# Attention decode on one core: the last K chunk loaded ahead of V, the last quarter of V multiplied in turned form, the output summed in one PSUM bank on four column groups

## Chip, cores and metric

One core of one Trainium2 chip. The metric is device time in microseconds (us) of the whole program; a run is one execution. Positions below are in us from the start of the span, which is the time from the first to the last instruction of the profiled execution and is some 1.8 us shorter than the reported time. Before the change the median of three runs was 1277.08 us (1277.07 to 1277.14).

Engines: PE does matrix products (PEld is its weight load), DVE is the vector engine, ACT the scalar engine, POOL the general one, and SP issues most DMAs ("SPq" is its queue).

## The reference, cut to what matters

```python
# x [1,1,448]; k_cache, v_cache [1, 8, 65536, 256] bf16; wq [448, 4096]; wo [4096, 448]
g = sigmoid((x * gate_w).sum(-1))
q = (x @ wq)                          # 16 heads of 256; two heads share one of 8 K/V heads
p = softmax(q . k * 256**-0.5)        # over 65536 positions
a = (p @ v).reshape(1, 1, 4096) @ wo  # [448]
b = mixer(layernorm(x))               # rank-one MLP, 14 blocks of 128 features, bias b2
out = g * a + (1 - g) * b
```

K and V are 268 MB each, and each byte is used once. Everything else is small.

## The kernel before

K and V of each head pair arrive in 8 chunks of 4 MB, K and V alternating, into a ring of four buffers, on SP's queue. Of a chunk, four steps of 1 MB: DVE turns (transposes) a K step, PE multiplies it with the query (8 products of 512 columns). After four steps ACT takes the exponential of the scores, DVE turns it, and PE multiplies V in 32 products, each with 4 columns of weights, on four column groups of PE that write four partition groups of one PSUM bank.

```python
    def load(item):                       # items: K0, V0, K1, V1, ... chunks of the stream
        ...
        elif item == 2 * total - 1:       # last K and V chunk: in pieces of SB = 16 blocks
            for s in range(last - 1):
                piece(item - 1, s * SB, SB)                     # K quarters 0, 1, 2
            piece(item, 0, SB)                                  # V quarter 0
            piece(item - 1, (last - 1) * SB, SB)                # K quarter 3
            for s in range(1, last - 1):
                piece(item, s * SB, SB)                         # V quarters 1, 2
            tail = SB // 2 - 2
            piece(item, (last - 1) * SB, SB - tail)             # V quarter 3, 10 blocks
            piece(item, last * SB - tail, tail)                 # and 6 blocks
    ...
    def p_v(i, s, lo=0, hi=SB // 2):      # 8 products for a V quarter
        ...
            nc.tensor.matmul(
                pv[g % 2][32 * a:32 * a + 4, :], lhsT=pT[:, k, :, s], rhs=vt[:, j * DH:(j + 2) * DH],
                start=first and k < 4, stop=last and k >= SB // 2 - 4, tile_position=(0, 32 * a))
    ...
    def o_scale(g):                       # evacuate and divide by the softmax sum
        nc.vector.tensor_scalar(out=pvs[:], in0=pv[g % 2][:], scalar1=rden[:, 0:1], ...)
    def o_turn(g):                        # add the four groups and turn: 4 fp32 products
        ...
        nc.vector.tensor_copy(out=oT[:], in_=o_ps)
    def o_out(g):                         # 4 products of 1x448, then added to an SBUF row by DVE
        ...
        nc.vector.tensor_tensor(out=dst[:], in0=acc[:], in1=a_ps, op=ALU.add)
    ...                                   # the end, after the last chunk's softmax
        for s in range(sizes[c]):
            p_v(i, s)                     # the last step in two parts, 10 and 6 blocks
        o_scale(HKV - 1)
    o_turn(HKV - 1)
    o_out(HKV - 1)
    nc.sync.dma_start(out=out[0, 0].rearrange("(o n) -> o n", o=1), in_=res[:])
```

(Comments are mine; the loop's end is shown with its conditions left out.) The mixer's 14 blocks run between the steps, each ending in one 1x448 product and one DVE accumulation into the same SBUF row.

The softmax here doesn't subtract the row's maximum and nothing guards it: scores larger than these inputs give would overflow.

## Time and profile before

| | before |
|---|---|
| time | 1277.08 us |
| span of the profiled run | 1275.1 us |
| HBM read | 544 MB, 427 GB/s over the span |
| PE, DVE busy | 59%, 52% |
| last byte of V landed | 1268.66 |
| last landing to end of span | 6.45 us |

The page divides the span into 40 equal slices; a digit of the DMA row is the busy share of the DMA engines in tenths, the GB/s row what they moved.

```profile
DMA  9999999999999999999999999999999999999996
GB/s 393 434 431 430 436 432 427 436 433 430 435 430 430 433 434 432 432 434 428 433 435 427 435 433 430 432 434 430 431 435 431 430 433 435 430 433 435 428 433 276
```

The stream is busy from start to end. Only the first and the last slice leave clear room, so a gain is to be looked for there first (a digit 9 means 90% or more, so this is a pointer and no proof). The end of the stream is the place to read closely. Here is the timeline of the kernel before. Columns: start, duration (both us), engine, line of the kernel, operation, output<-inputs, partitions x elements out<-in, how many instructions the row merges; in brackets, how long the engine sat idle before it and what released it.

```profile
1260.91 2.31 DVE L346 STREAM_TRANSPOSE kT_184<-ring_72 128x2048 f32<-128x2048 f32 x1 [1.36 <-DMA ring_72<-in_A_k_cache_dram]
1263.28 1.89 PE L354 MATMUL sc_75<-kT_184,qw 128*128 128x512 bf16 x8 [1.78 <-DVE kT_184 L346]
...
1265.21 0.60 ACT L361 ACTIVATE p_186<-sc_75 128x512 bf16<-128x512 f32 x1 [12.98 <-PE sc_75 L354]
...
1265.93 0.71 DVE L365 STREAM_TRANSPOSE pT_188<-p_186 128x512 bf16<-128x512 bf16 x1 [2.71 <-ACT p_186 L361]
...
1267.05 2.04 PE L376 MATMUL pv_77<-ring_73,pT_188 128*4 128x512 bf16 x32
...
1268.71 0.09 PEld L376 LDWEIGHTS <-pT_188 128*4 128x4 bf16 x2 [0.26 <-issue]
1269.14 0.75 DVE L393 TENSOR_SCALAR pvs<-pv_77,rden 128x512 f32<-128x512 f32 x1 [1.61 <-PE pv_77 L376]
...
1269.94 1.05 PE L402 MATMUL misc<-sel,pvs 128*128 128x2 f32 x8 [0.85 <-DVE pvs L393]
1271.03 0.16 DVE L406 CAST oT<-misc 128x4 bf16<-128x4 f32 x1 [1.15 <-PE misc L402]
...
1271.25 0.92 PE L412 MATMUL misc<-wo_97,oT 128*1 128x448 bf16 x4 [0.25 <-DVE oT L406]
1272.20 0.61 DVE L417 TENSOR_TENSOR res<-acc,misc 1x448 bf16<-1x448 f32 x1 [1.01 <-PE misc L412]
1272.84 0.32 SPq L452 DMA_DIRECT2D out_dram<-res  x1
```

Read it downwards. The last K quarter is turned as soon as it lands (1260.91, released by the DMA), its scores, exponential and turn follow, and the 32 products with V start at 1267.05. The last two weight loads (1268.71) come after a pause, 0.05 us after the last V blocks landed (1268.66, below). The view names no releaser here; that they waited for these blocks is read from the times. From there everything is in series: scaling, turn (8 passes), cast, four products, addition, output DMA.

Each DMA of 128 partitions is spread over 16 rings and its semaphore is raised once by each. From these records in the trace, for each piece of the last chunk, when the fastest and the slowest ring had landed it (a consumer that needs the whole piece waits for the slowest):

```
piece            before: fastest, slowest   after: fastest, slowest
K quarter 3          1253.49  1260.79          1251.16  1258.77
V quarter 0          1251.00  1258.32          1253.64  1261.23
V quarter 1          1255.93  1263.79          1256.09  1263.67
V quarter 2          1258.37  1266.22          1258.52  1266.24
V quarter 3, end     1260.85  1268.66          1261.01  1268.68
```

### The profile page before, as it was taken

How to read it: one execution, taken by the hardware profiler on the slowest of the kernel's cores; microseconds unless marked ns; L12 is line 12 of the kernel's file. 1: busy time of each engine (PE TensorE's matmuls, PEld its weight loads, DVE VectorE, ACT ScalarE, POOL GpSimd, SP SyncE). 2: the span in 40 equal slices, each digit the busy share in tenths (PEclk: the TensorE clock that was granted, in tenths of full speed). 3: DMA queues.
4: the chain of work that ended last, by engine and by line, in shares of the span. 5: the costliest groups of instructions: out<-in, count | busy, mean ns of one | idle time of the engine just before them, and what ended most of it. 6: DMA issues, size and time to landing. Idle time of an engine off the chain costs nothing.

```text
span 1275.1 us, 10091 instructions
## 1 busy us (share of the span) xinstructions
PE 758.4 (59%) x4374; PEld 288.1 (23%) x4374; DVE 661.7 (52%) x429; ACT 62.7 (5%) x159; POOL 83.1 (7%) x118
## 2 busy tenths in 40 slices
PE   3564656655566556656557565575655655656656
PEld 2121222212222222222122122221222222222212
DVE  7364455554464644646445455464453644545545
ACT  0000000000000000000000000000000000000000
POOL 3111012110021100210000000000000000000000
PEclk9888888888889887898888888788887888879789
DMA  9999999999999999999999999999999999999996
GB/s 393 434 431 430 436 432 427 436 433 430 435 430 430 433 434 432 432 434 428 433 435 427 435 433 430 432 434 430 431 435 431 430 433 435 430 433 435 428 433 276
DMA packets 21154, 544.88 MB, mean 427 GB/s; under 512 B 2675, under 2 KB 2806, under 8 KB 3958
## 3 DMA queue, kind: packets, MB, share of 16 engines
q1 hardware_dynamic: 19730, 540.55, 98.5%
q0 software_dynamic: 1376, 3.69, 0.8%
q8 instruction: 34, 0.56, 0.2%
q14 instruction: 10, 0.08, 0.0%
q10 hardware_dynamic: 4, 0.00, 0.0%
HBM read 544.22 MB, written 0.00 MB: 427 GB/s over the span
## 4 chain that ended last, share of the span: by engine, by line
DMA 64%; DVE 17%; PE 17%; issue 2%; DVEq 0%; SPq 0%; ACT 0%; ACTq 0%
DMA ring_70<-in_A_k_cache_dram 58%; PE sc_74 L354 14%; DVE kT_183 L346 9%; DVE kT_184 L346 7%; DMA ring_72<-in_A_k_cache_dram 6%; PE sc_75 L354 1%; PE misc L402 1%; DVE acc L337 1%; PE misc L412 1%; PE misc L325 0%; DVE acc L417 0%; PE pv_77 L376 0%; DVE pT_188 L365 0%; DVE oT L406 0%; DVEq L346 0%
## 5 line engine op out<-in xcount | busy, mean ns | idle before, releaser
L354 PEld LDWEIGHTS <-qw 128*128 128x128 bf16 x2048 | 222.3, 111 | 772.5 <-issue 324.5
L354 PE MATMUL sc_74<-kT_183,qw 128*128 128x512 bf16 x512 | 190.8, 536 | 239.6 <-DVE kT_183 L346 239.6
L346 DVE STREAM_TRANSPOSE kT_183<-ring_70 128x2048 f32<-128x2048 f32 x64 | 147.6, 2306 | 166.6 <-DMA ring_70<-in_A_k_cache_dram 146.7
L354 PE MATMUL sc_75<-kT_183,qw 128*128 128x512 bf16 x512 | 145.7, 433 | 114.7 <-DVE kT_183 L346 114.7
L346 DVE STREAM_TRANSPOSE kT_183<-ring_72 128x2048 f32<-128x2048 f32 x64 | 147.0, 2297 | 114.3 <-DMA ring_72<-in_A_k_cache_dram 91.7
L354 PE MATMUL sc_74<-kT_184,qw 128*128 128x512 bf16 x512 | 150.9, 445 | 25.4 <-DVE kT_184 L346 25.4
L346 DVE STREAM_TRANSPOSE kT_184<-ring_72 128x2048 f32<-128x2048 f32 x64 | 145.7, 2277 | 4.9 <-PE sc_75 L354 3.4
L346 DVE STREAM_TRANSPOSE kT_184<-ring_70 128x2048 f32<-128x2048 f32 x64 | 145.6, 2275 | 2.8 <-PE sc_74 L354 2.7
L354 PE MATMUL sc_75<-kT_184,qw 128*128 128x512 bf16 x512 | 131.7, 401 | 18.1 <-DVE kT_184 L346 18.1
L365 DVE STREAM_TRANSPOSE pT_187<-p_185 128x512 bf16<-128x512 bf16 x32 | 22.8, 712 | 103.4 <-ACT p_185 L361 103.4
L365 DVE STREAM_TRANSPOSE pT_188<-p_186 128x512 bf16<-128x512 bf16 x32 | 22.8, 712 | 86.7 <-ACT p_186 L361 86.7
L361 ACT ACTIVATE p_185<-sc_74 128x512 bf16<-128x512 f32 x32 | 19.1, 597 | 713.4 <-PE sc_74 L354 713.4
L376 PE MATMUL pv_77<-ring_71,pT_187 128*4 128x512 bf16 x512 | 30.4, 379 | 24.4 <-DVE pT_187 L365 24.4
L376 PE MATMUL pv_76<-ring_71,pT_187 128*4 128x512 bf16 x512 | 30.4, 379 | 24.4 <-DVE pT_187 L365 24.4
L376 PEld LDWEIGHTS <-pT_187 128*4 128x4 bf16 x1024 | 22.1, 86 | 87.3 <-DVE pT_187 L365 64.6
L376 PE MATMUL pv_77<-ring_73,pT_188 128*4 128x512 bf16 x512 | 30.6, 379 | 18.3 <-DVE pT_188 L365 18.3
L376 PE MATMUL pv_76<-ring_73,pT_188 128*4 128x512 bf16 x512 | 30.4, 379 | 18.3 <-DVE pT_188 L365 18.3
L361 ACT ACTIVATE p_186<-sc_75 128x512 bf16<-128x512 f32 x32 | 19.1, 597 | 449.5 <-PE sc_75 L354 449.5
L376 PEld LDWEIGHTS <-pT_188 128*4 128x4 bf16 x1024 | 22.1, 86 | 71.5 <-DVE pT_188 L365 48.4
L337 DVE SCALAR_TENSOR_TENSOR acc<-misc,half_g,acc 1x448 f32<-1x448 f32 x14 | 9.4, 672 | 53.1 <-PE misc L325 53.1
L314 POOL TENSOR_SCALAR t_b<-t_b 128x448 f32<-128x448 f32 x14 | 7.9, 567 | 361.3 <-ACT t_b L306 361.3
L139 POOL DMA_DIRECT2D wo_97<-in_A_wo_dram x4 | 3.1, 784 | 295.4 <-PE misc L412 295.4
(90 smaller groups left out, 201.9 us busy)
## 6 DMA issues: line engine op xcount, KB each, us to landing
ring_70<-in_A_k_cache_dram SPq DMA_DIRECT2D x32, 4096.0 KB, 26.5
ring_71<-in_A_v_cache_dram SPq DMA_DIRECT2D x32, 4096.0 KB, 29.8
ring_72<-in_A_k_cache_dram SPq DMA_DIRECT2D x31, 4096.0 KB, 29.4
ring_73<-in_A_v_cache_dram SPq DMA_DIRECT2D x31, 4096.0 KB, 33.9
ring_72<-in_A_k_cache_dram SPq DMA_DIRECT2D x4, 1024.0 KB, 27.5
ring_73<-in_A_wq_dram SPq DMA_DIRECT2D x1, 3072.0 KB, 10.4
ring_73<-in_A_v_cache_dram SPq DMA_DIRECT2D x3, 1024.0 KB, 26.9
wo_96<-in_A_wo_dram POOLq DMA_DIRECT2D x4, 448.0 KB, 15.1
```

The costliest lines, as they stand in the source:

```text
L139: nc.gpsimd.dma_start(out=wo_t[g % 2][:], in_=A_wo[g * 512:(g + 1) * 512, :].rearrange("(q p) n -> p q n", p=128),)
L314: nc.gpsimd.tensor_scalar(out=t_b[:], in0=t_b[:], scalar1=GELU_C1, scalar2=1.0, op0=ALU.mult, op1=ALU.add)
L337: nc.vector.scalar_tensor_tensor(out=acc[:], in0=misc[0:1, 0:D], scalar=half_g[0:1, 0:1], in1=acc[:], op0=ALU.mult, op1=ALU.add,)
L346: nc.vector.transpose(out=kT[n % 2][:].bitcast(FP32), in_=kn[:, s * SB * 128:(s + 1) * SB * 128])
L354: nc.tensor.matmul(sc[i % 2][:], lhsT=qw[:, g, q, PAD - s:PAD - s + 128], rhs=kv[:, :, q // 2, :, q % 2], start=(s == 0 and q == 0), stop= ...
L361: nc.scalar.activation(out=p_t[i % 2][:], in_=sc[i % 2][:], func=ACT.Exp, scale=scale, accum_out=den[g % 2][:, c:c + 1],)
L365: nc.vector.transpose(out=pT_t[i % 2][:], in_=p_t[i % 2][:])
L376: nc.tensor.matmul(pv[g % 2][32 * a:32 * a + 4, :], lhsT=pT[:, k, :, s], rhs=vt[:, j * DH:(j + 2) * DH], start=first and k < 4, stop=last ...
L402: nc.tensor.matmul(o_ps[:, 2 * c:2 * c + 2], lhsT=pvs[:, lo:lo + 128], rhs=sel[:, 2 * half:2 * half + 2], start=(half == 0), stop=(half == 1),
L412: nc.tensor.matmul(a_ps, lhsT=oT[:, 2 * c + r:2 * c + r + 1], rhs=wo_t[g % 2][:, 2 * r + c, :], start=(c == 0 and r == 0), stop=(c == 1 an ...
```

## The change

Intent: the work behind the last V byte should be as short as possible. Five things were done.

1. All of the last K chunk is loaded ahead of V.
2. The last V quarter is multiplied the other way round ("turned"): V's blocks are the weights (128x128) and the two heads' probabilities the two moving columns. The result comes out already turned, and is added in PSUM to the turned sums of all earlier V. So evacuation and turn of the earlier sums can run before the last V quarter lands.
3. Division by the softmax sum moves behind the turn, onto 128x4 values.
4. The output row is summed all along in one PSUM bank, as four rows of 112 in four column groups, so the DVE accumulations go. The bias is broadcast early and added once at the end, and four rows are written out.
5. Query windows are built for one head pair at a time (a smaller clearing at the start).

```diff
@@ load @@
-            for s in range(last - 1):
+            for s in range(last):
                 piece(item - 1, s * SB, SB)
-            piece(item, 0, SB)
-            piece(item - 1, (last - 1) * SB, SB)
-            for s in range(1, last - 1):
+            for s in range(last - 1):
                 piece(item, s * SB, SB)
-            tail = SB // 2 - 2
-            ... 10 and 6 blocks
+            piece(item, (last - 1) * SB, SB - TAIL)      # TAIL = 4
+            piece(item, last * SB - TAIL, TAIL)
@@ gate: the bias rides along in the second column @@
-    nc.tensor.matmul(z_ps, lhsT=one_f[:], rhs=z1[:], start=True, stop=True)
+    nc.tensor.matmul(z_ps, lhsT=one_f[:], rhs=zb[:], start=True, stop=True)
@@ output sum @@
+    def to_acc(col, rows, stop=False):
+        for a in range(4):
+            nc.tensor.matmul(
+                acc[32 * a:32 * a + 1, 0:DQ], lhsT=col, rhs=rows[:, DQ * a:DQ * (a + 1)],
+                start=a not in opened, stop=stop, tile_position=(0, 32 * a),
+            )
+            opened.add(a)
@@ last V quarter @@
+    def p_v_turned(i, s, lo, hi):
+        ...
+        for j in range(lo, hi):
+            for c in range(2):
+                at = (s * SB + j) * DH + c * 128
+                nc.tensor.matmul(
+                    o_ps[:, 2 * c:2 * c + 2], lhsT=vt[:, at:at + 128], rhs=pT[:, j, :, s],
+                    start=False, stop=(j == SB - 1 and c == 1), skip_group_check=True,
+                )
@@ end @@
-    o_turn(HKV - 1)
-    o_out(HKV - 1)
-    nc.sync.dma_start(out=out[0, 0].rearrange("(o n) -> o n", o=1), in_=res[:])
+    nc.vector.tensor_copy(out=pvs[:, 0:DH], in_=pv[g % 2][:, 0:DH])
+    nc.scalar.activation(out=pvs[:, DH:2 * DH], in_=pv[g % 2][:, DH:2 * DH], func=ACT.Copy)
+    o_turn(g)
+    p_v_turned(i, s, 0, SB - TAIL)
+    p_v_turned(i, s, SB - TAIL, SB)
+    nc.vector.tensor_tensor(oT, o_ps, rden, op=ALU.mult)          # 128x4, views left out
+    o_out(g)
+    nc.vector.tensor_scalar(
+        out=res[0:97, :], in0=acc[0:97, 0:DQ], scalar1=bias[0:97, 0:1], scalar2=None, op0=ALU.add
+    )
+    nc.sync.dma_start(out=out[0, 0].rearrange("(a n) -> a n", a=4), in_=res[0:97:32, :])
```

(Cut: the per-head softmax sum, the smaller query windows, and the same steps between head pairs.)

## The prediction

> **What bounds the kernel now.** The page shows 544 MB read at a mean 427 GB/s and DMA at 9 tenths in each of the 40 slices but the last (6 tenths). PE is busy 59%, DVE 52% of the 1275.1 us span. Changes in steady state hide under the stream; only what lies before the first and after the last byte moves the time.
>
> **Head.** The removed 7.04 us clearing of the query window comes before the first K tile, for which DVE still waits at 23.25 us (timeline). I expect nothing.
>
> **Tail of before** (landing records, timeline). The last K quarter lands at 1260.8 and starts a chain: transpose 2.3, scores 1.9, exp 0.7, transpose 0.7 us, then all 32 products with V from 1267.05. The last V blocks land on the slowest engine at 1268.7, so chain and stream end together. Then in series: last products and drain 0.43, scaling of 128x512 0.75, turn 1.05, cast 0.17, four 1x448 products 0.93, addition 0.61, output DMA 2.27, some 0.05 per hand-over: 6.4 us from last landing to end.
>
> **What the change does there.** The last K quarter goes ahead of V0 and lands 2.4 us earlier (1 MB at 427 GB/s); three quarters of V are multiplied as they land, and their evacuation and turn no longer wait for the last bytes. Estimate from the durations above, from the landing of the third V quarter (1266.2, same place in the stream):
> - 8 products and drain 0.8 -> 1267.05
> - DVE copies one half, 128x256: 0.46 (between 0.17 for 128x4 and 0.75 for 128x512) -> 1267.55. ACT copies the other only afterwards (the program makes it wait), under the first half's turn. The Trainium skill, page "PSUM — Partial Sum Buffer", section "PSUM bank collisions raise a hardware error", says why: two engines must not use one bank and quadrant at once.
> - turn 1.05 -> 1268.6
> - 32 turned products (128x128 weights, 2 columns) 0.88, from the query projection's 27.5 ns per pair, drain 0.15 -> 1269.65
> - scaling into oT 0.2 -> 1269.85
> - 16 products of 1x112 in four column groups 0.65, against 0.93. At 28 ns a pair issue limits: the skill's page "TensorEngine Tiling (Array Packing)", section "Instruction Overhead", gives about 60 cycles per matmul, which agrees with 27.5 ns
> - bias addition 97x112 0.3, against 0.61 -> 1270.85
> - output DMA of four 224-byte rows 2.3 -> 1273.1
>
> That is 2.0 us off the span, all on the critical path, all in the last 10 us. The path moves from the stream's last byte to PE's work after the third V quarter: the last 4 blocks (1268.7) are there when PE reaches them.
>
> Off the path, worth nothing: 21 DVE accumulations of 0.6 to 0.7 us removed, scaling moved to ACT, query windows built per head pair, 324 more PE instructions.
>
> **Predicted: 1275.1 us, range 1274.2 to 1276.3.** Chances: faster by over 2% 0.01, within 2% 0.985, slower 0.005. Before spreads over 0.07 us, so a 2 us gain should be visible.
>
> **Right if** the slices' GB/s are unchanged; the last landing stays near 1268.7; the turn starts before it; the last eight turned products wait for no DMA; last landing to end is 4.2 to 4.8 us instead of 6.4. **Wrong if** turned products cost 50 ns or more a pair (+0.7 us); the column groups do not overlap (over 0.9 us); the four-row output is slower than 2.3 us; PE is through before the last blocks land (0.5 us better); or the stream itself ends earlier or later: 0.1% of it is 1.3 us, as large as the effect.

## The result, and the profile after

| | before | after |
|---|---|---|
| time, median of four runs | 1277.11 us (1277.07 to 1278.43) | 1275.60 us (1275.12 to 1276.39) |
| ratio | | 0.9986, 95% interval 0.9969 to 1.0004 |
| span of the profiled run | 1275.1 | 1273.5 |
| last V landing | 1268.66 | 1268.68 |
| last landing to end of span | 6.45 | 4.80 |

Ratios are the mean time of one kernel's fast runs over the mean of the other's fast runs of the same rounds, so not quite the ratio of the medians quoted. The interval just includes 1, but the change was run in two more batches (below). Over the three batches its 14 runs lie between 1275.05 and 1276.39 us, the 23 runs of before between 1276.77 and 1278.43, with no overlap.

The same lines of the page, after: the stream is as it was.

```profile
DMA  9999999999999999999999999999999999999997
GB/s 400 422 438 429 431 435 431 432 431 437 430 428 436 433 429 431 436 430 434 433 433 428 435 433 430 432 432 434 432 434 429 434 429 434 437 429 433 434 429 300
```

And the timeline of the kernel after, from the last K chunk on:

```profile
1253.09 8.85 DVE L351 STREAM_TRANSPOSE kT<-ring 128x2048 f32<-128x2048 f32 x4
...
1261.99 1.90 PE L359 MATMUL sc<-kT,qw 128*128 128x512 bf16 x8 [0.29 <-DVE kT L351]
...
1264.65 0.71 DVE L370 STREAM_TRANSPOSE pT<-p 128x512 bf16<-128x512 bf16 x1 [2.71 <-ACT p L366]
...
1265.77 1.47 PE L382 MATMUL pv<-ring,pT 128*4 128x512 bf16 x24
...
1267.29 0.42 DVE L472 COPY pvs<-pv 128x256 f32<-128x256 f32 x1 [0.98 <-PE pv L382]
1267.75 0.38 ACT L473 ACTIVATE pvs<-pv 128x256 f32<-128x256 f32 x1 [3.14 <-DVE pvs L472]
...
1267.77 1.05 PE L414 MATMUL misc<-sel,pvs 128*128 128x2 f32 x8 [0.53 <-DVE pvs L472]
...
1268.69 0.97 PE L425 MATMUL misc<-pT,ring 128*128 128x2 bf16 x32
1269.69 0.16 DVE L477 TENSOR_TENSOR oT<-misc,rden 128x4 bf16<-128x4 f32 x1 [1.98 <-PE misc L425]
...
1269.91 0.37 PE L314 MATMUL acc<-wo,oT 128*1 128x112 bf16 x16 [0.25 <-DVE oT L477]
1270.33 0.33 DVE L482 TENSOR_SCALAR res<-acc,bias 97x112 bf16<-97x112 f32 x1 [0.48 <-PE acc L314]
1270.69 0.65 SPq L485 DMA_DIRECT2D out_dram<-res  x1
```

DVE turns the four last K quarters one after the other, without a pause (1253.09, 8.85 us). The 24 plain products now start at 1265.77, and the evacuation starts before the last V landing at 1268.68. PE goes from the turn straight into the 32 turned products, with no wait for the last blocks. The tail compares as follows (starts of the rows shown, before and after):

| step | before | after | difference | predicted after |
|---|---|---|---|---|
| last landing to start of cast or scaling into oT | 2.37 | 1.01 | -1.36 | 0.95 |
| that to start of addition (final products) | 1.17 | 0.64 | -0.53 | 0.85 |
| addition to issue of the output | 0.64 | 0.36 | -0.28 | 0.3 |
| issue of the output to end of span | 2.27 | 2.79 | +0.52 | 2.3 |
| sum | 6.45 | 4.80 | -1.65 | 4.4 |

At the head, one thing was new. In the timeline of the kernel after, PE waits for the small bias load (`zb`), and the query projection waits behind it:

```profile
20.86 0.55 PE L227 MATMUL misc<-zb,one_f 1*128 1x2 f32 x2 [14.82 <-DMA zb<-in_B_b_dram]
```

The load of the second V chunk, which needs the projection's buffer, was issued at 26.07, against 18.77 in before.

### The profile page after: what moved, and what is told of

The parts are those of the page before. It is cut to its first block, busy times and chain, and to the rows that moved or that the text cites. A ratio compares the mean times of both kernels' runs of the same rounds, so it can differ in the third digit from the quotient of the medians.

```text
span 1273.5 us, 10437 instructions
## 1 busy us (share of the span) xinstructions
PE 745.4 (59%) x4536; PEld 286.0 (22%) x4536; DVE 642.1 (50%) x396; ACT 70.1 (6%) x181; POOL 73.2 (6%) x117
## 4 chain that ended last, share of the span: by engine, by line
DMA 70%; DVE 13%; PE 13%; issue 3%; POOL 0%; DVEq 0%; ACT 0%; POOLq 0%
DMA ring<-in_A_k_cache_dram 69%; DVE kT L351 12%; PE sc L359 12%; DMA zb<-in_B_b_dram 1%; PE misc L414 1%; PE pv L382 0%; DVEq L351 0%; ACT p L366 0%; PE misc L425 0%; DVE pT L370 0%; DVE h_bc L257 0%; POOL w1T L132 0%; POOL rstd L247 0%; PE misc L227 0%; POOL b1T L134 0%
## 5 line engine op out<-in xcount | busy, mean ns | idle before, releaser
L359 PE MATMUL sc<-kT,qw 128*128 128x512 bf16 x2048 | 604.6, 453 | 403.9 <-DVE kT L351 403.5
L351 DVE STREAM_TRANSPOSE kT<-ring 128x2048 f32<-128x2048 f32 x256 | 580.1, 2295 | 429.2 <-DMA ring<-in_A_k_cache_dram 326.6
L382 PE MATMUL pv<-ring,pT 128*4 128x512 bf16 x2040 | 121.4, 379 | 86.2 <-DVE pT L370 86.2
L370 DVE STREAM_TRANSPOSE pT<-p 128x512 bf16<-128x512 bf16 x64 | 45.5, 712 | 174.2 <-ACT p L366 174.2
L366 ACT ACTIVATE p<-sc 128x512 bf16<-128x512 f32 x64 | 38.2, 597 | 1064.2 <-PE sc L359 1064.2
L382 PEld LDWEIGHTS <-pT 128*4 128x4 bf16 x2040 | 44.0, 86 | 159.1 <-DVE pT L370 113.9
L336 POOL TENSOR_TENSOR t_b<-t_b,u_b 128x448 f32<-128x448 f32 x14 | 16.0, 1144 | 1.2
L343 POOL TENSOR_TENSOR gel<-t_b,u_b 128x448 bf16<-128x448 f32 x14 | 15.8, 1126 | 1.2
L366 ACT ACTIVATION_READ_ACCUMULATOR p<-sc 128x1 f32 x64 | 12.4, 194 | 0.0
L414 PEld LDWEIGHTS misc<-sel,pvs 128*128 128x128 f32 x64 | 11.0, 243 | 3.5 <-issue 1.9
```

Of the source, the lines that this page charges most:

```text
L336: nc.gpsimd.tensor_tensor(out=t_b[:], in0=t_b[:], in1=u_b[:], op=ALU.mult)
L343: nc.gpsimd.tensor_tensor(out=gel[:], in0=t_b[:], in1=u_b[:], op=ALU.mult)
L351: nc.vector.transpose(out=kT[n % 2][:].bitcast(FP32), in_=kn[:, s * SB * 128:(s + 1) * SB * 128])
L359: nc.tensor.matmul(sc[i % 2][:], lhsT=qw[g % 2][:, q, PAD - s:PAD - s + 128], rhs=kv[:, :, q // 2, :, q % 2], start=(s == 0 and q == 0), s ...
L366: nc.scalar.activation(out=p_t[i % 2][:], in_=sc[i % 2][:], func=ACT.Exp, scale=scale, accum_out=den[g % 2][:, c:c + 1],)
L370: nc.vector.transpose(out=pT_t[i % 2][:], in_=p_t[i % 2][:])
```

## The experiments

Theory A: the gain comes only from the last 10 us, and it needs two parts together. In the profiled execution of before, the chain of the last K quarter and the last V bytes arrive at the scaling at the same moment. The new order frees one, the turned form the other. Rivals: the order of loading alone did it (the chain of waits of before runs through the last K quarter); the turned form alone did it; or the stream itself became faster. The first four runs are made for this, all on one chip with the same nine runs of before.

| run | median us | range | ratio to before (95%) |
|---|---|---|---|
| before | 1277.32 | 1276.77 to 1277.65 | |
| after_again | 1275.20 | 1275.07 to 1275.79 | 0.9986 (0.9974 to 0.9999) |
| reorder_only | 1277.22 | 1276.75 to 1279.03 | 1.0000 (0.9987 to 1.0014) |
| late_k | 1277.29 | 1276.75 to 1277.47 | 1.0000 (0.9987 to 1.0012) |
| plain_last | 1276.32 | 1276.16 to 1276.86 | 0.9994 (0.9982 to 1.0007) |

### The change once more

No edit.

> The changed kernel once more, for a tight ratio and as the base of the next three. Theory A (all of the gain is in the last 10 us): ratio to before 0.9987, about 1.6 us less; last V landing within 0.1 us of that of before (about 1268.7 us of span), landing to end 4.8 us against 6.45. Rival B (the gain came with the stream, by chance or by fewer interruptions): the ratio moves by more than 0.0005 from 0.9987 and the landing moves with it.

The ratio was 0.9986 again, the last landing at 1268.66 again as in before. The stream did not move, so rival B falls. Landing to end was 5.28 us in this profile, not 4.80: PE's chain was 0.27 us later and the final products ran longer (0.54 instead of 0.37 us). The clock records show why: the granted PE clock fell to half at 1270.0. More on this below.

### Only the order of loading

```diff
# the kernel before
-            for s in range(last - 1):
+            for s in range(last):
                 piece(item - 1, s * SB, SB)
-            piece(item, 0, SB)
-            piece(item - 1, (last - 1) * SB, SB)
-            for s in range(1, last - 1):
+            for s in range(last - 1):
                 piece(item, s * SB, SB)
```

> The kernel before with one thing changed: all four quarters of the last K tile are loaded ahead of the first V quarter. Theory A: in before two branches ended together, the last K quarter's chain with its 32 products (1269.1) and the last V landing plus two products (1268.7 + 0.43); so the order alone is worth nothing: within 0.3 us of before. The last K quarter lands at 1258.8 instead of 1260.8, the first product with V starts about 1265.8 instead of 1267.05, and the last products wait for the DMA; scaling still starts at about 1269.1. Rival C (the chain of waits of before runs through the last K quarter, so its order is the gain): 1.2 us or more off the time.

The time equals before's (1277.22 against 1277.32). Its timeline shows PE freed from the K chain and waiting for V instead:

```profile
1268.37 0.59 PE L374 MATMUL pv<-ring,pT 128*4 128x512 bf16 x5 [0.82 <-DMA ring<-in_A_v_cache_dram]
...
1269.30 0.39 PE L374 MATMUL pv<-ring,pT 128*4 128x512 bf16 x3 [0.34 <-DMA ring<-in_A_v_cache_dram]
...
1269.73 0.75 DVE L391 TENSOR_SCALAR pvs<-pv,rden 128x512 f32<-128x512 f32 x1 [3.19 <-PE pv L374]
...
1270.54 1.86 PE L400 MATMUL misc<-sel,pvs 128*128 128x2 f32 x8 [0.85 <-DVE pvs L391]
...
1272.66 1.65 PE L410 MATMUL misc<-wo,oT 128*1 128x448 bf16 x4 [0.26 <-DVE oT L404]
```

The last K quarter landed at 1258.64 and the first products started at 1266.07. Then came two waits for V, 0.82 and 0.34 us, the second for the last piece, which landed at 1269.26 in this execution. The scaling started at 1269.73 and not at the expected 1269.1, because of this landing: from landing to scaling it is 0.47 us, and was 0.48 in before. Rival C falls: a step through which the chain of waits runs is not worth its length if a second branch ends with it.

This profiled execution was the slowest of the five, 1279.03 us. In it the turn took 1.86 us (1.05 in before) and the final products 1.65 (0.92): the granted clock was 0.5 from 1270.44 on.

### The change with the old order of loading

```diff
# the kernel after
-            for s in range(last):
+            for s in range(last - 1):
                 piece(item - 1, s * SB, SB)
-            for s in range(last - 1):
+            piece(item, 0, SB)
+            piece(item - 1, (last - 1) * SB, SB)
+            for s in range(1, last - 1):
                 piece(item, s * SB, SB)
```

> The changed kernel with the old order of loading (first V quarter ahead of the last K quarter). Theory A: the turned form needs the early K: products with V start at 1267.05, 24 of them end at 1268.55, then copy, turn and 32 turned products in series, so the scaling into oT starts at 1271.0 instead of 1269.7: 1.3 us more than the changed kernel, 0.3 us less than before. Rival D (the turned form alone is the gain): no more than 0.3 us above the changed kernel.

2.1 us more than the change by the medians, where I had expected 1.3: the whole gain was gone. Rival D falls.

```profile
1261.75 2.31 DVE L353 STREAM_TRANSPOSE kT<-ring 128x2048 f32<-128x2048 f32 x1 [1.51 <-DMA ring<-in_A_k_cache_dram]
...
1267.90 1.47 PE L384 MATMUL pv<-ring,pT 128*4 128x512 bf16 x24
...
1271.82 0.16 DVE L479 TENSOR_TENSOR oT<-misc,rden 128x4 bf16<-128x4 f32 x1 [1.97 <-PE misc L427]
```

In this execution the last K quarter landed at 1261.63, not 1260.79 as in before's profile, so the chain and all behind it came about 0.8 us later than I had assumed. That accounts for the size in this profile. Why the median is also 0.8 us above the expectation is not shown in full; one profile is one execution. Part of it lies in the expectation: the piece at this place in the stream landed between 1260.86 and 1261.64 in the 13 other profiles (median 1261.22), so the 1260.79 that I built on was the earliest of all, some 0.4 us early.

### The change with a plain last V quarter

```diff
# the kernel after; p_v takes lo and hi again, and its stop flag the last step
-        for s in range(sizes[c] - (i == total - 1)):
+        for s in range(sizes[c] - (i == total - 1)):      # V quarters 0 to 2 as they were
             p_v(i, s)
     ...
+    p_v(i, s, 0, (SB - TAIL) // 2)
+    p_v(i, s, (SB - TAIL) // 2)
     nc.vector.tensor_copy(out=pvs[:, 0:DH], in_=pv[g % 2][:, 0:DH])
     ...
     o_turn(g)
-    p_v_turned(i, s, 0, SB - TAIL)
-    p_v_turned(i, s, SB - TAIL, SB)
```

> The changed kernel with the last V quarter multiplied in the plain form like the others, in two pieces (12 and 4 blocks), and evacuation and turn after the last of it. Everything else of the change stays. Theory A: evacuation starts at 1269.1 (last landing 1268.7 plus two products), then copy 0.45 and turn 1.05: the scaling into oT starts at 1270.7 instead of 1269.7: 1.0 us more than the changed kernel. Rival C (order of loading is the gain): as fast as the changed kernel within 0.3 us.

1.1 us more than the change by the medians, as expected.

```profile
1269.00 0.42 DVE L473 COPY pvs<-pv 128x256 f32<-128x256 f32 x1 [2.28 <-PE pv L381]
...
1270.57 0.16 DVE L476 TENSOR_TENSOR oT<-misc,rden 128x4 bf16<-128x4 f32 x1 [1.15 <-PE misc L413]
```

With the last landing at 1268.53, the evacuation starts at 1269.00 and the scaling into oT at 1270.57: 2.04 us from landing to scaling, against 1.01 in the change's first profile and 1.30 in its repetition. Rival C falls again.

Together the runs show theory A in part. The order alone is worth nothing; everything but the order is worth nothing; everything but the turned last quarter is worth 1.0 us, the whole 2.1 us (medians of this batch). So all of the gain needs the order, but only about half of it needs the turned form. How the other 1.0 us divides among the rest (the halved evacuation, the final steps) these runs do not show; one_group below gives a part of it. The sizes are rough: the same change was worth 1.5, 2.1 and 1.3 us by the medians of the three batches.

The second group ran on another chip, sharing nine runs of before (median 1276.95, 1276.82 to 1277.42). The change itself was run on that chip with the third group: 1275.68.

| run | median us | range | ratio to before (95%) |
|---|---|---|---|
| one_group | 1276.18 | 1275.90 to 1276.80 | 0.9994 (0.9980 to 1.0008) |
| split_k62 | 1275.34 | 1275.14 to 1276.37 | 0.9989 (0.9977 to 1.0002) |
| two_queues | 1276.00 | 1275.80 to 1276.31 | 0.9992 (0.9980 to 1.0005) |
| bf16_turn | 1274.99 | 1274.51 to 1275.38 | 0.9984 (0.9972 to 0.9997) |

### One column group instead of four

```diff
-    DQ = D // 4
+    DQ = D
@@ to_acc @@
-        for a in range(4):
+        for a in range(1):
@@ end: one row added and written @@
-        out=res[0:97, :], in0=acc[0:97, 0:DQ], scalar1=bias[0:97, 0:1], ...
+        out=res[0:1, :], in0=acc[0:1, 0:DQ], scalar1=bias[0:1, 0:1], ...
-        out=out[0, 0].rearrange("(a n) -> a n", a=4), in_=res[0:97:32, :]
+        out=out[0, 0].rearrange("(a n) -> a n", a=1), in_=res[0:1, :]
```

> The changed kernel with its output sum on one column group (one row of 448, as before) instead of four groups of 112; still summed all along in the PSUM bank. Theory A (two effects that nearly cancel): final products 0.93 instead of 0.40 us, bias addition about 0.55 instead of 0.33, but output DMA of one row 2.27 from issue to end instead of 2.79: in sum 0.2 to 0.3 us more than the changed kernel (1275.2). Rival E (the four groups are an independent part of the gain): 0.7 us more or worse.

0.5 us more than the change on the same chip (1276.18 against 1275.68, ranges just overlapping), between my two figures, so neither is met.

```profile
1270.21 1.26 PE L314 MATMUL acc<-wo,oT 128*1 128x448 bf16 x4 [0.25 <-DVE oT L477]
1271.51 0.67 DVE L482 TENSOR_SCALAR res<-acc,bias 1x448 bf16<-1x448 f32 x1 [1.36 <-PE acc L314]
1272.21 0.32 SPq L485 DMA_DIRECT2D out_dram<-res  x1
```

From the scaling (1270.00) to the end of the span (1274.48) it is 4.48 us; in the change's first repetition it is 3.98 (1269.96 to 1273.94). The two clocks are not quite alike: here the fall to half came at 1270.65, amid the final products, there at 1270.00, before them. The sum of the steps: final products 1.26 against 0.54, addition 0.67 against 0.33, output DMA 2.27 against 2.81. So the four groups are worth about half a microsecond net in these profiles, after paying 0.5 us for the four-row output.

### The K chunk before the last in quarters

```diff
+        if item == 2 * total - 4:
+            for s in range(sizes[-2]):
+                piece(item, s * SB, SB)
-        if item < 2 * total - 2:
+        elif item < 2 * total - 2:
```

> The changed kernel with the K tile before the last loaded in quarters too, so that DVE starts on it some 7 us earlier. In the changed kernel DVE begins the last K tile at 1253.1 although its first quarter landed at 1251.5, and runs its four transposes without a pause. Theory F (the changed kernel's path comes through DVE's backlog on the last two K tiles, and the third V quarter's landing stands 0.25 us behind it): products with V start at about 1265.1 instead of 1265.8, evacuation at 1267.05 instead of 1267.3: 0.25 us less. Rival G (K alone is the limit): 0.6 us or more less. Rival H (the last landing is the limit): nothing.

Inconclusive. The median was 1275.34 against 1275.68 of the change on that chip, but the ranges overlap, and the profile shows that the intended thing did not happen. DVE was rid of its backlog and waited for the K data (5.69 us), but PE then held it up. First DVE, then PE:

```profile
1251.96 2.31 DVE L354 STREAM_TRANSPOSE kT<-ring 128x2048 f32<-128x2048 f32 x1 [5.69 <-DMA ring<-in_A_k_cache_dram]
...
1257.69 4.51 DVE L354 STREAM_TRANSPOSE kT<-ring 128x2048 f32<-128x2048 f32 x2 [0.92 <-PE sc L362]
```

```profile
1254.33 5.06 PE L362 MATMUL sc<-kT,qw 128*128 128x512 bf16 x16 [1.30 <-DVE kT L354]
```

The 16 score products took 5.06 us; the granted clock was 0.5 from 1247.01 to 1257.24. Products with V started at 1266.03, not at the expected 1265.1. In the 13 other profiles the slow spell nearest to this place was over by 1246.8; whether the edit moved it is not shown. So theory F and its rivals are not told apart by this run.

### Two queues for the output

```diff
-    nc.sync.dma_start(out=out[0, 0].rearrange("(a n) -> a n", a=4), in_=res[0:97:32, :])
+    halves = out[0, 0].rearrange("(a n) -> a n", a=4)
+    nc.sync.dma_start(out=halves[0:2, :], in_=res[0:33:32, :])
+    nc.scalar.dma_start(out=halves[2:4, :], in_=res[64:97:32, :])
```

> The changed kernel with its four output rows written by two DMAs, two rows each, from two engines' queues. In the changed kernel the issue took 0.65 us and landed 1.65 us after it started; in before, one row, 0.32 and 1.12. If the extra 0.5 us is issue time that grows with the rows: 0.25 to 0.35 us less than the changed kernel. If it is a fixed cost of more than one row, or of the landing: no change within 0.1 us, or worse.

No gain: 1276.00, 0.3 us above the change, with ranges that overlap.

```profile
1271.12 0.63 SPq L486 DMA_DIRECT2D out_dram<-res  x1
1271.12 0.59 ACTq L487 DMA_DIRECT2D out_dram<-res  x1
```

An issue of two rows took 0.63 and 0.59 us, as long as one of four rows (0.65), and twice as long as one of one row (0.32). So the extra did not grow from two rows to four. That fits a fixed cost of having more than one row; whether the two issues, made at the same time, held each other up was not tested. From issue to end it was 2.98 us, against 2.79 with one DMA. The Trainium skill, page "DMA: Bandwidth & Descriptors", section "Issuing engines are not separate DMA queues", says that issuing on several engines saves only the sequencer's time; this run agrees, and here not even that was saved.

### The turn in bf16

```diff
-    pvs = work.tile([128, 512], FP32, name="pvs")
+    pvs = work.tile([128, 512], BF16, name="pvs")
+    sel_b = const.tile([128, 4], BF16)                  # a bf16 copy of sel
@@ o_turn @@
-        ... rhs=sel[:, 2 * half:2 * half + 2]
+        ... rhs=sel_b[:, 2 * half:2 * half + 2]
```

> The changed kernel with the evacuated sums (and the selector) in bf16 instead of fp32, so the turn is 4 single-pass products instead of 8 passes. Theory F: the turn takes 0.2 us instead of 1.05; PE then meets the last landing (1268.7) rather than arriving 0.15 us late with 32 products still to do: scaling into oT starts at about 1269.1 instead of 1269.7, 0.5 to 0.6 us less than the changed kernel. Rival H (the last landing is already the limit): nothing. Rival I (the path is the DMA chain further on): nothing.

0.7 us less than the change on that chip by the medians (1274.99 against 1275.68, ranges overlapping); the output was still correct. The turn no longer sets the pace; ACT's half of the evacuation does:

```profile
1268.34 0.20 PE L416 MATMUL misc<-sel_b,pvs 128*128 128x2 bf16 x2 [0.21 <-ACT pvs L475]
...
1268.40 0.97 PE L427 MATMUL misc<-pT,ring 128*128 128x2 bf16 x32
1269.40 0.16 DVE L479 TENSOR_TENSOR oT<-misc,rden 128x4 bf16<-128x4 f32 x1 [1.54 <-PE misc L427]
```

The scaling started at 1269.40, not at 1269.1: the last landing (1268.30) was no limit in this execution; 32 turned products took 0.97 us in one go. That the change's path runs through PE's work and not through the last byte is seen best across the profiles. From the first product with V to the scaling it is 3.92 us in each of the change's three (3.48 here, so the turn gave 0.44), while the last landing came 2.91, 2.62 and 2.79 us after that first product and moved nothing. Rivals H and I fall. The rest of the 0.7 us between the profiles of after_third and this kernel is an earlier K chain (0.15 us) and a clock that fell only after the final products (0.37 us against 0.54).

The third group ran on the same chip as the second; its ten runs of before (median 1276.98) include those nine.

| run | median us | range | ratio to before (95%) |
|---|---|---|---|
| after_third | 1275.68 | 1275.05 to 1276.00 | 0.9989 (0.9975 to 1.0003) |
| bias_apart | 1275.62 | 1275.36 to 1276.68 | 0.9991 (0.9979 to 1.0004) |
| best_b | 1274.75 | 1274.55 to 1275.46 | 0.9983 (0.9970 to 0.9995) |
| best_c | 1274.79 | 1274.66 to 1274.98 | 0.9983 (0.9969 to 0.9996) |

### The change a third time

No edit.

> The changed kernel again, on the chip of the next three. 1.7 us less than before, within 0.4 us: the oT scaling starts between 1269.6 and 1270.0, and its final products take 0.37 us if the granted clock is still full then, 0.54 if it has been halved.

1.3 us less than before by the medians, at the lower edge of what I expected. The scaling started at 1269.99, final products took 0.54 us, the clock had fallen at 1269.85.

### The bias apart from the gate

```diff
-    nc.tensor.matmul(z_ps, lhsT=one_f[:], rhs=zb[:], start=True, stop=True)
+    nc.tensor.matmul(z_ps[:, 0:1], lhsT=one_f[:], rhs=zb[:, 0:1], start=True, stop=True)
     ... gate, query projection, query windows ...
+    nc.tensor.matmul(z_ps[:, 1:2], lhsT=one_f[:], rhs=b2[:], start=True, stop=True)
+    nc.vector.tensor_tensor(out=bias[:], in0=z_ps[:, 1:2], in1=gate[:, 1:2], op=ALU.mult)
     load(RING - 1)
```

> The changed kernel with the output bias broadcast by a product of its own, after the query projection, as a scalar apart from the gate. In the changed kernel the gate's product carries the bias along and so waits for its small load until 21.7 us, and the query projection behind it on PE with it; the second V tile's load is issued at 26.1 us instead of 18.8. Theory A (hidden: the queue holds work until about 37 us): within 0.3 us of the changed kernel, although the projection starts some 10 us earlier. Rival J (the late head costs time that the tail's gain covers up): 0.5 us or more less.

The load of the second V chunk was issued at 15.80 instead of 26.07, and the time stayed: 1275.62 against 1275.68. The wait at the head is real and hidden. Rival J falls.

### The third V quarter turned too, under the evacuation

```diff
# on top of the bf16 turn
-        for s in range(sizes[c] - (i == total - 1)):
+        for s in range(sizes[c] - 2 * (i == total - 1)):
             p_v(i, s)                                # plain: V quarters 0 and 1 only
     ... evacuation by DVE and ACT ...
-    o_turn(g)
+    p_v_turned(i, s - 1, 0, SB, True)                # opens the bank
+    o_turn(g, False)                                 # adds to it
     p_v_turned(i, s, 0, SB - TAIL)
```

> The changed kernel with the turn in bf16 and the third V quarter in turned form as well, run on PE ahead of the turn of the evacuated sums, so that PE multiplies while DVE and ACT evacuate. Theory F: 16 plain products 1.0, 32 turned 0.9, turn 0.2, 32 turned 0.95 after 1265.9: the path meets the last landing, scaling into oT at 1269.0 to 1269.2 instead of 1269.7 to 1270.0; 0.6 to 0.8 us less than the changed kernel, 0.3 less than with the bf16 turn alone. Rival I: nothing beyond the bf16 turn alone.

> The same with the bias apart as well. Theory A: as fast as the one before within 0.2 us. Rival J: 0.5 us less.

0.9 us less than the change on the same chip (1274.75 and 1274.79 against 1275.68), 0.2 less than the bf16 turn alone, though these two ranges overlap. The second kernel's profile shows the end that I was after:

```profile
1267.89 1.01 PE L429 MATMUL misc<-pT,ring 128*128 128x2 bf16 x32 [0.37 <-DMA ring<-in_A_v_cache_dram]
1268.94 0.16 DVE L482 TENSOR_TENSOR oT<-misc,rden 128x4 bf16<-128x4 f32 x1 [2.10 <-PE misc L429]
```

PE waits for the DMA of the 12-block piece, which landed at 1267.85, ahead of the last 32 products (0.37 us), and the scaling starts 0.45 us after the last landing (1268.49). In the first kernel's profile the K chain was late (its 16 products started at 1266.46), and the scaling started at 1269.52, later than the expected 1269.0 to 1269.2. These two are the fastest kernels.

## Why the prediction was right

1275.1 us was predicted, with a range of 1274.2 to 1276.3; 1275.60 was measured, 1.5 us less than before in the median, where 2.0 was predicted. The place (the last 10 us) and the mechanism (evacuation and turn taken out from behind the last byte) were right. The entry to the path was wrong and three terms were mis-sized. That the end of the span still came within 0.4 us (1273.1 predicted, 1273.48 in the first profile) is in part luck: the evacuation began 0.24 us late and the output took 0.49 us more, while turn with turned products took 0.18 us and final products 0.21 us less. Two of the prediction's own tests were not passed: the four-row output was to take no more than 2.3 us, and the time from last landing to end was to be 4.2 to 4.8 us, but was 4.80, 5.28 and 5.10 in the change's three profiles. And before did not spread over 0.07 us, as three runs had it, but over 1.66 us in 23. Point by point:

- "Changes in steady state hide under the stream": right. Last landing at 1268.66 and 1268.68; three profiles of the change agree within 0.2 us.
- "The last K quarter goes ahead of V0 and lands 2.4 us earlier": 2.0 earlier. But the products with V started only 1.28 us earlier (1267.05 to 1265.77), since in the change DVE was still busy with the quarters before: the quarter landed at 1258.77 and its turn started at 1259.67 (chain of waits).
- "three quarters of V are multiplied as they land": wrong. The chain of the scores came later than two of these landings, so all 24 products ran in one go after it, and the evacuation began at 1267.29 instead of 1267.05. The path starts at the K chain and not at the third V landing.
- Copy, turn, turned products: predicted 0.5, 1.05 and 1.03; measured 0.48 (1267.29 to 1267.77), 1.05 and 0.86 (1268.83, where the turn ends in the chain, to 1269.69). The single starts of the turned products in the trace are 26 ns apart, near the 27.5 assumed; the first began at 1268.69, while the turn was still ending. The last eight waited for no DMA, as stated. ACT's half of the evacuation began only when DVE's was done (1267.75), as the page "PSUM — Partial Sum Buffer" leads to expect, and was hidden under the turn.
- "16 products of 1x112 in four column groups 0.65": mis-sized. 0.37 us, 0.42 to the start of the addition. My figure had 28 ns of issue for each of 16 pairs and 0.2 us of drain. The single starts in the trace show that the issue term was wrong: four products, one for each column group, start within 10 ns, and the rounds of four start 48 ns apart (some 90 ns in after_again, once the clock had fallen to half). The last round starts 0.145 us after the first, and its products are recorded as 0.21 us long, so the drain is there. The page "TensorEngine Tiling (Array Packing)", section "Instruction Overhead", gives about 60 cycles a matmul (estimate: 25 ns at the 2.4 GHz that the page "TensorE: Matmul & The Clock Gate", section "What's actually happening", gives); within a round, with 3 ns between starts, this overhead is not paid for each product, so "issue limits" was wrong here.
- "output DMA of four 224-byte rows 2.3": mis-sized. 2.79 us. This is the largest error of a single term, +0.5 us. It was partly offset by the term before. By the prediction's own list ("the four-row output is slower than 2.3 us") this step failed.
- "Head ... I expect nothing": right in effect (bias_apart), but I had not seen that the gate's product waits for the bias, so the projection started some 7 us later than before. Slack hid it (estimate: the 16.3 MB queued ahead of the delayed load last some 38 us at 427 GB/s, and it was issued at 26).
- What the prediction lacked: the granted PE clock at the end. In the profiles it fell to half between 1268.5 and 1272.8. Where PE's tail was still running then, it stretched (final products 0.54 instead of 0.37, since the rounds after the fall are twice as far apart; in the slowest run of reorder_only the turn 1.86 instead of 1.05). This was seen in single profiles; how much of the spread between runs it makes is not shown.

## What to carry to other kernels

Where a stream bounds the kernel, cost the tail as several branches that meet: taking the work of one branch away is worth only the distance to the next (here nothing for the order of loading alone, and nothing for all the rest without it). Put everything that does not need the last bytes ahead of them, in a form to which the last bytes can still be added: a turned product that accumulates in PSUM does this for a reduction followed by a transpose. And cost the output store too: splitting a result over four partitions to speed up the last product made the store 0.5 us longer here.

## What the Trainium skill lacked or had wrong

- "DMA: Bandwidth & Descriptors" gives no cost by the number of rows for a small store issued from SP. Here one row of 896 bytes took 0.32 us to issue and 1.12 us from issue to its last landing; four rows of 224 bytes 0.65 and 1.65; two rows from each of two queues 0.63 and 0.59 to issue, 1.57 and 1.83 to land. Its section "Why a DMA increments its semaphore by 16 and not by 1" says that the sequencer writes the increments of the unused rings immediately; here the first record, read as that write, came 0.44 us (one row) and 1.02 us (four rows) after the start of the issue. It came 0.68 and 0.56 us before the first landing, so it waited for no data, but with four rows it stood 0.37 us after the end of the issue.
- The same page gives no figure for how far the rings drift apart under a long stream: at the end of this one, the slowest of 16 rings landed a piece 7.3 to 8.4 us after the fastest, and the figure changed by about 1 us from run to run, and in three of the 14 profiles by 0.6 to 0.9 us within the last chunk. A consumer that waits for the whole piece sees the slowest.
- "TensorE: Matmul & The Clock Gate", section "What's actually happening", describes a half clock after an idle window of 3413 ns and the full clock after a busy one. The records agree in the two values (0.5 and 1.0) and in the grain (slow spells of 3.41, 6.83, 10.24 and 13.65 us), and for all falls but the last of each profile they fit idleness: PE had records for at most 1.5 of the 3.41 us before. The last falls do not fit it so plainly: in after_again the clock fell at 1270.0 although PE had records for all but some 0.6 us of the 3.4 us before. These were small products (4 columns of weights, or 2 moving columns); whether such work counts as little work was not tested.
- On the tail of a kernel, no page says that a fall of the clock there can cost as much as the change under study: 0.8 us in the turn and 0.7 us in the final products of one execution.
